# The last batch's q loaded by two transfers of eight outer parts, in a kernel of sliding-window attention and a spectral mix

## The chip, the cores and the metric

The kernel runs on one core of a Trainium2 chip. The metric is the time of one execution on the device in microseconds (us). The core has engines that work side by side: TensorE (PE; its weight loads are listed as PEld), VectorE (DVE), ScalarE (ACT), GpSimd (POOL) and SyncE (SP), and sixteen DMA engines that move data between HBM and the core's memories.

## What is computed

The first part is causal attention in a window of 64 positions, for 8 batches, 8 heads, 576 positions and a head dimension of 64:

```python
scores = (1 / sqrt(D)) * q @ k.transpose(0, 1, 3, 2)
mask = (rel >= 0) & (rel < 64)                 # rel = query position - key position
attn = softmax(where(mask, scores, -1e9))
x = (attn @ v).transpose(0, 2, 1, 3).reshape(B, S, H * D)
```

The second part mixes x in the spectrum of its 64 lowest modes, with one complex 512x512 matrix for each mode:

```python
X = rfft(x, axis=1)[:, :64]
Yr = einsum("bmd,mde->bme", Xr, w_r) - einsum("bmd,mde->bme", Xi, w_i)
Yi = einsum("bmd,mde->bme", Xr, w_i) + einsum("bmd,mde->bme", Xi, w_r)
u = x + irfft(Y, n=576, axis=1)
out = u + maximum(u @ w_ch, 0)
```

The matrices of the modes are 127 matrices of 512x512 in fp32 (the imaginary one of mode 0 isn't needed), by far most of what is read.

## The kernel before

**Stages.** Attention is worked in 36 windows of 512 columns and ends at about 140 us. Between the windows each batch's k, v and q are transposed on TensorE into the layout that the scores need. From 141 us on the 127 matrices are multiplied in, one "half" (16 matmuls, L618) after the other, and between them TensorE does the channel product of x, later the first modes' part of the inverse transform and its product. After the last half the late modes' part is added, rectified and stored (from 390 us).

**The loads.** All loads but one (k of batch 0, on SP) are issued from POOL, which converts them from fp32 to bf16 on the way: `load` (L109) for q, k and v, `load_w` and `load_two` (L136, L141) for one or two matrices. The order is fixed: `refill` (L402) issues, when a batch's k, v or q has been transposed, the load of the same tensor two batches on, and a matrix into each place that is free. Once attention is over, `issue` (L567) loads matrices into a ring of places as they come free. Eight transfers of POOL can be on their way at once: an issue waits until the one eight before it has landed.

**The layout of q, k and v.** Of a batch, [8 heads, 576, 64], each head's 576 positions are cut into 32 runs of RUN = 18 positions. `runs` (L106) gives 128 partitions of two pieces: partition 32*g + p holds run p of head g and of head g + 4. A piece is 18 x 64 = 1,152 elements, 4,608 bytes read, 2,304 written. So a load is one transfer of 256 rows with an outer dimension of 128. The tile `rq` has two buffers; the last batch's q is issued after the q of batch 5 has been transposed.

**The transposes.** `part` (L242) transposes six of the 18 positions of all runs, for both pieces, into a PSUM tile of [128, 6, 128], and a copy (`evac`, L55, on ACT or DVE) puts the columns where they belong: column 32*g + p of position c goes to place g*576 + 18*p + c. `transpose_units` (L234) lists a batch's twelve units of work; those of q are the seventh to ninth, and they run after those of k and v.

Of the kernel before, what the change touches and what calls it, by code (L numbers as in the profile page):

```python
# [11 lines left out]
BF16 = mybir.dt.bfloat16  # L12
# [8 lines left out]
def view(ap, off, dims):  # L21

    return bass.AP(ap.tensor, ap.offset + off, [list(ap.ap[0])] + [list(d) for d in dims])
# [3 lines left out]
def kernel(  # L27
# [10 lines left out]
    nc = tc.nc  # L38
    B, H, S, D = q.shape
# [8 lines left out]
    RUN = S // 32  # L48
# [6 lines left out]
    def evac(o, i, on_act):  # L55

        if on_act:
            return nc.scalar.copy(out=o, in_=i)  # L58
        return nc.vector.tensor_copy(out=o, in_=i)  # L59
# [30 lines left out]
    acons = p1.enter_context(tc.tile_pool(name="acons", bufs=1, side="right"))  # L90
# [10 lines left out]
    RAW = {"k": k, "q": q, "v": v}  # L101

    def raw_tile(which):
        return rawp.tile([128, 2, RUN * D], BF16, name="r" + which)

    def runs(b, which):  # L106
        return RAW[which][b].rearrange("(x g) (p c) d -> (g p) x (c d)", g=4, c=RUN)

    def load(b, which):  # L109
        r = raw_tile(which)  # L110
        nc.gpsimd.dma_start(out=r, in_=runs(b, which))
        raws[b, which] = r


# [63 lines left out]
    with tc.manual_schedule(engines=ALL_FOUR):  # L178
# [3 lines left out]
        with tc.tile_pool(name="tmpf", bufs=1, side="right") as tmp:  # L182
            mo = tmp.tile([128, NM], FP32, name="mo")
            to = tmp.tile([128, NT], FP32, name="to")
            nc.gpsimd.iota(mo, pattern=[[1, NM]], base=0, channel_multiplier=0,
                           allow_small_or_imprecise_dtypes=True)
            nc.gpsimd.iota(to, pattern=[[128, NT]], base=0, channel_multiplier=1,
                           allow_small_or_imprecise_dtypes=True)
            nc.gpsimd.memset(ident, 0.0)
            nc.gpsimd.affine_select(out=ident, in_=ident, compare_op=ALU.not_equal, fill=1.0,  # L190
                                    base=0, pattern=[[-1, 128]], channel_multiplier=1)
            load(0, "q")
            load(0, "v")
            for t0, t1 in ((0, 3), (3, NT)):
                n = t1 - t0
                mt = tmp.tile([128, 2, n * NM], FP32, name="mtf")
                nc.vector.tensor_tensor(out=view(mt, 0, [[NM, n], [1, NM]]), in0=view(mo, 0, [[0, n], [1, NM]]),
                                        in1=view(to, t0, [[1, n], [0, NM]]), op=ALU.mult)
                gen_trig(tmp, mt, n * NM, trigF[:, t0:t1, 0:NM], trigF[:, t0:t1, NM:2 * NM], "f")
                if t0 == 0:  # L200
                    nc.vector.tensor_copy(out=ident_bf, in_=ident)
        nc.scalar.activation(out=spark, in_=ident[:, 0:1], func=ACT_F.Exp)
        raws[0, "k"] = raw_tile("k")
        for c, engine in enumerate((nc.vector, nc.gpsimd, nc.vector)):
            cc = slice(6 * D * c, 6 * D * (c + 1))
            engine.tensor_copy(out=raws[0, "k"][:, :, cc], in_=k_first[:, :, cc])
        load(1, "k")
        for i in range(4):
            half = i % 2
# [24 lines left out]
    def transpose_units(b):  # L234

        rk, rq, rv = (raws.pop((b, which)) for which in "kqv")
        qT = qtp.tile([128, 4, S], BF16, name="qT")
        vT = vtp.tile([128, 4, S], BF16, name="vT")
        kT, vt = kTs[b % 2], vts[b % 2]
        qTs[b] = qT  # L240

        def part(src, dst, c0, on_act):  # L242
            def f():
                ps = ps_misc.tile([128, 6, 128], BF16, name="pst", tag="misc")
                for c in range(6):
                    for hh in range(2):
                        nc.tensor.transpose(out=ps[64 * hh:64 * hh + 64, c, :],  # L247
                                            in_=src[:, hh, (c0 + c) * D:(c0 + c + 1) * D],
                                            identity=ident_bf)
                evac(view(dst, c0, [[S, 4], [RUN, 32], [1, 6]]),  # L250
                     view(ps, 0, [[32, 4], [1, 32], [128, 6]]), on_act)
            return f

        def vback(u):
            def f():
                ps = ps_misc.tile([128, 6, 128], BF16, name="psv", tag="misc")
                for i in range(6):
                    a, j = divmod(6 * u + i, 9)
                    if j == 4:
                        parts = [(0, 64, 2 * a, 512), (64, 64, 2 * a + 1, 0)]  # L260
                    else:
                        parts = [(0, 128, 2 * a + (j > 4), 128 * j - (j > 4) * S)]
                    for r0, n, g, t0 in parts:
                        nc.tensor.transpose(out=ps[r0:r0 + n, i, :],  # L264
                                            in_=vT[:, g, t0:t0 + n], identity=ident_bf)
                evac(view(vt, 6 * u * VW, [[18 * VW, 2], [VW, 6], [1, D]]),
                     view(ps, 0, [[D, 2], [128, 6], [1, D]]), u != 1)
                if u:
                    hs = slice(u - 1, u + 2, 2)
                    nc.vector.tensor_copy(out=vt[64:128, 1, hs, 1:9], in_=vt[64:128, 0, hs, 0:8])  # L270
                    nc.vector.tensor_copy(out=vt[0:64, 1, hs], in_=vt[0:64, 0, hs])
            return f

        return [part(rk, kT, 0, True), part(rk, kT, 6, False), part(rk, kT, 12, True),
                part(rv, vT, 0, False), part(rv, vT, 6, True), part(rv, vT, 12, False),
                part(rq, qT, 0, True), part(rq, qT, 6, False), part(rq, qT, 12, True),
                vback(0), vback(1), vback(2)]

    def head_of(n):
# [143 lines left out]
    with tc.manual_schedule(engines=ALL_FOUR):  # L423
        first = transpose_units(0)
        for j in (0, 1, 2, 6, 7, 8):
            first[j]()
            refill(0, j)
            if j in (2, 8):
                warm_up(3)
        for half in range(2):  # L430
            pp = slice(64 * half, 64 * half + 64)
            nc.vector.tensor_copy(out=band2[pp], in_=band[pp, half, :])
        mask(0, 1)
        scores(0)
        for j in (3, 4, 5):
            first[j]()
            refill(0, j)
            warm_up(2)
        for vt in vts:
            nc.vector.memset(vt[:, 0, :, :, 64:66], 1.0)  # L440
        for j in (9, 10, 11):
            first[j]()
            refill(0, j)
        nc.vector.memset(pso, 1.0)
        nc.vector.tensor_copy(out=ident_r, in_=ident)
    with tc.manual_schedule(engines={E.PE, E.Pool}):
# [9 lines left out]
        def unit(b, j):  # L456
            if b not in units:
                units[b] = transpose_units(b)
            units[b][j]()
            refill(b, j)  # L460
            turned(b, j)

        for w in range(NWIN + 1):
# [5 lines left out]
            n = len(todo)  # L469
# [16 lines left out]
            if w in (NWIN - 4, NWIN - 1):  # L486
                i = (B - 2) % 2 if w == NWIN - 4 else (B - 1) % 2
                spare(kTs[i])
                spare(qtp.tile([128, 4, S], BF16, name="qT"))
            if w in (NWIN - 4, NWIN):  # L490
                i = (B - 2) % 2 if w == NWIN - 4 else (B - 1) % 2
# [363 lines left out]
    def step(f, *a, delta=0):  # L855
        n = {add_z: 2, make_u: 4, last_tile: 2 + (a[-1] is True)}.get(f, 0)
        items.append((lambda: f(*a), delta, n, f is last_tile))
# [20 lines left out]
    for k, (f, delta, n, few) in enumerate(items):  # L878
        i = S_I + k * (T_I - 2 - S_I) // len(items)
# [25 lines left out]
    with tc.manual_schedule(engines=ALL_FOUR):  # L905
# [92 lines left out]
        for k in range(6):  # L998
# [10 lines left out]
                              in_=view(psys[0], 0, [[2 * B, NC], [2, B], [1, 2]]))  # L1009
# [78 lines left out]
```

## Time and profile before

| | us |
|---|---|
| median of 3 runs | 425.43 |
| the runs | 425.22, 425.43, 598.11 |
| profiled execution | 425.65 |
| its span | 423.8 |
| PE busy | 352.3 (83%) |
| DVE busy | 189.2 (45%) |
| ACT busy | 159.8 (38%) |
| POOL busy | 81.6 (19%) |

The span goes from the first instruction to the last; the profiled execution's own time is 1.85 us more. A busy share is an average over stages with different limits. A view names an instruction by its engine, the line of the code and the tiles that it writes and reads (`wms<-in_moe_w_r_dram` is a load of matrices into the tile wms). Queue q0 holds the transfers issued from POOL, q1 those from SP, q8 the fetches of instructions. The 16 DMA engines' busy time is given as a share; packets of one engine overlap a little, so a full stretch shows slightly over 1.

The trace also holds, for each transfer, sixteen reports of landing, one from each DMA engine, in the order of time; they don't tell which engine sent them. Four transfers, first report and the others from it (us):

| transfer, issued at | first report | eighth | ninth | last |
|---|---|---|---|---|
| rq, batch 0, 1.60 | 8.46 | +0.2 | +0.2 | +0.7 |
| rq, batch 7, 87.78 | 104.44 | +0.5 | +1.4 | +2.4 |
| wls, 190.59 | 207.56 | +0.9 | +3.1 | +4.5 |
| wms, the last, 375.98 | 384.51 | +1.0 | +4.6 | +5.9 |

### The profile page before, as it was taken

How to read it: one execution, taken by the hardware profiler on the slowest of the kernel's cores; microseconds unless marked ns; L12 is line 12 of the kernel's file. 1: busy time of each engine (PE TensorE's matmuls, PEld its weight loads, DVE VectorE, ACT ScalarE, POOL GpSimd, SP SyncE). 2: the span in 40 equal slices, each digit the busy share in tenths (PEclk: the TensorE clock that was granted, in tenths of full speed). 3: DMA queues.
4: the chain of work that ended last, by engine and by line, in shares of the span. 5: the costliest groups of instructions: out<-in, count | busy, mean ns of one | idle time of the engine just before them, and what ended most of it. 6: DMA issues, size and time to landing. Idle time of an engine off the chain costs nothing.

```text
span 423.8 us, 11438 instructions
## 1 busy us (share of the span) xinstructions
PE 352.3 (83%) x5156; PEld 233.6 (55%) x5185; DVE 189.2 (45%) x359; ACT 159.8 (38%) x267; POOL 81.6 (19%) x146
## 2 busy tenths in 40 slices
PE   7799999999997779866669587767789899998994
PEld 3466656656654567644446455545556565554451
DVE  6676775766764001634332351121104345340895
ACT  5565766767754100122102110110023343330863
POOL 6322222221031130411112012120121112200000
PEclk9999999999999555966756656666579999999997
DMA  8999999999999999999999999999999999995598
GB/s 212 211 214 212 214 212 212 213 213 213 214 214 214 213 215 261 215 214 214 215 214 213 215 213 215 215 213 215 213 215 214 214 213 211 214 214 106 203 370 320
DMA packets 29920, 92.55 MB, mean 218 GB/s; under 512 B 2352, under 2 KB 2352, under 8 KB 29872
## 3 DMA queue, kind: packets, MB, share of 16 engines
q0 software_dynamic: 24624, 81.21, 95.9%
q1 hardware_dynamic: 5248, 10.62, 6.8%
q8 instruction: 40, 0.66, 0.6%
q14 instruction: 8, 0.07, 0.0%
HBM read 162.53 MB, written 9.44 MB: 406 GB/s over the span
## 4 chain that ended last, share of the span: by engine, by line
PE 42%; DMA 39%; DVE 7%; issue 5%; ACT 3%; POOL 0%; DVEq 0%; POOLq 0%; ACTq 0%
DMA wms<-in_moe_w_r_dram 20%; DMA wms<-in_moe_w_i_dram 19%; PE psy L618 7%; PE pso L343 6%; PE pst L247 5%; PE psv L264 3%; PE psx L365 3%; PE pss L963 3%; DVE x_sb L351 2%; PE pss L956 2%; PE pss L300 2%; PE pss L319 2%; PE psy L903 2%; DVE vT L59 2%; PE psf L800 1%
## 5 line engine op out<-in xcount | busy, mean ns | idle before, releaser
L759 PE MATMUL psz<-wch,xT 128*128 128x512 f32 x144 | 65.0, 594 | 0.0
L753 DVE CAST xT<-pxt 128x1024 fp32r<-128x1024 bf16 x18 | 22.0, 1224 | 78.0 <-PE pxt L748 78.0
L762 ACT CAST Z<-psz 128x1024 fp32r<-128x1024 f32 x18 | 18.2, 1012 | 102.2 <-PE psz L759 94.5
L325 ACT ACTIVATE et<-pss 128x512 bf16<-128x512 f32 x72 | 39.2, 599 | 13.7 <-PE pss L319 13.7
L618 PE MATMUL psy<-XQ,wls 128*128 128x16 bf16 x560 | 22.0, 192 | 23.7 <-DMA wls<-in_moe_w_r_dram 14.2
L759 PEld LDWEIGHTS psz<-wch,xT 128*128 128x128 f32 x144 | 37.4, 287 | 5.9
L618 PE MATMUL psy<-XQ,wms 128*128 128x16 bf16 x624 | 25.1, 192 | 17.9 <-DMA wms<-in_moe_w_i_dram 12.7
L618 PEld LDWEIGHTS <-wls 128*128 128x128 bf16 x560 | 19.5, 106 | 33.8 <-DMA wls<-in_moe_w_r_dram 17.4
L618 PEld LDWEIGHTS <-wms 128*128 128x128 bf16 x624 | 21.4, 103 | 30.2 <-DMA wms<-in_moe_w_i_dram 15.3
L343 PE MATMUL pso<-vt,et 128*64 128x65 bf16 (+1 forms) x576 | 32.3, 203 | 3.5 <-DVE x_sb L351 1.6
L811 DVE TENSOR_TENSOR Z<-pse,Z 128x1024 fp32r<-128x1024 f32 x16 | 19.6, 1225 | 29.3 <-PE pse L800 29.3
L343 PEld LDWEIGHTS <-et 128*64 128x64 bf16 (+1 forms) x576 | 22.2, 109 | 14.2 <-issue 6.7
L351 DVE TENSOR_TENSOR x_sb<-pso,rcp 128x640 bf16<-128x640 f32 x32 | 26.3, 822 | 0.9
L618 PE MATMUL psy<-XQ,wt 128*128 128x16 bf16 x560 | 20.5, 192 | 4.8 <-DMA wt<-in_moe_w_i_dram 2.3
L618 PEld LDWEIGHTS <-wt 128*128 128x128 bf16 x560 | 18.3, 104 | 11.2 <-DMA wt<-in_moe_w_i_dram 4.3
L59 DVE CAST YT<-psy 128x256 fp32r<-128x256 f32 x6 | 2.5, 424 | 42.0 <-PE psy L618 32.7
L59 DVE COPY vT<-pst 128x768 bf16<-128x768 bf16 x16 | 15.3, 958 | 12.9 <-PE pst L247 11.3
L981 ACT ACTIVATE pss<-pss 128x512 f32<-128x512 f32 x35 | 18.5, 581 | 4.7 <-PE pss L963 4.1
L300 PE MATMUL pss<-band,ident_bf 64*64 64x512 bf16 x120 | 16.5, 396 | 0.0
L264 PE MATMUL psv<-ident_bf,vT 128*128 128x128 bf16 (+1 forms) x160 | 15.6, 226 | 0.6 <-DVE vT L59 0.6
L58 ACT COPY vt<-psv 128x768 bf16<-128x768 bf16 x16 | 12.9, 807 | 8.3 <-PE psv L264 8.2
L58 ACT COPY qT<-pst 128x768 bf16<-128x768 bf16 x16 | 12.9, 813 | 6.4 <-PE pst L247 6.4
(191 smaller groups left out, 605.7 us busy)
## 6 DMA issues: line engine op xcount, KB each, us to landing
wt<-in_moe_w_i_dram POOLq DMA_DIRECT2D x19, 512.0 KB, 20.4
wt<-in_moe_w_r_dram POOLq DMA_DIRECT2D x16, 512.0 KB, 19.4
wls<-in_moe_w_r_dram POOLq DMA_DIRECT2D x8, 1024.0 KB, 21.8
wms<-in_moe_w_i_dram POOLq DMA_DIRECT2D x7, 1024.0 KB, 22.2
wms<-in_moe_w_r_dram POOLq DMA_DIRECT2D x7, 1024.0 KB, 21.6
wls<-in_moe_w_i_dram POOLq DMA_DIRECT2D x6, 1024.0 KB, 21.3
rq<-in_q_dram POOLq DMA_DIRECT2D x8, 576.0 KB, 15.3
rv<-in_v_dram POOLq DMA_DIRECT2D x8, 576.0 KB, 13.8
```

What stands on the lines that cost most here:

```text
L58: return nc.scalar.copy(out=o, in_=i)
L59: return nc.vector.tensor_copy(out=o, in_=i)
L247: nc.tensor.transpose(out=ps[64 * hh:64 * hh + 64, c, :], in_=src[:, hh, (c0 + c) * D:(c0 + c + 1) * D], identity=ident_bf)
L264: nc.tensor.transpose(out=ps[r0:r0 + n, i, :], in_=vT[:, g, t0:t0 + n], identity=ident_bf)
L300: nc.tensor.matmul(out=pss[(2 * w + hh) % 3][64 * half:64 * half + 64, :], lhsT=ident_bf[pp, pp], rhs=view(band[pp], 128 * half, [[0, WIN ...
L325: nc.scalar.activation(out=et[:, hh, :], in_=pss[(2 * w + hh) % 3], func=ACT_F.Exp, scale=EX_SCALE)
L343: nc.tensor.matmul(out=pso[po, hh, block(b, i // 2) * VW:block(b, i // 2) * VW + D + 1], lhsT=et[pk, hh, col:col + 64], rhs=vt[pk, 1 - f % ...
L351: nc.vector.tensor_tensor(out=view(x_sb, b * NT * DM + g * D, [[4 * D, 2], [DM, NT], [1, D]]), in0=view(pso, 0, [[512, 2], [VW, NT], [1, D]]),
L618: nc.tensor.matmul(out=view(psy, off + 2 * B * e, [[1, 2 * B]]), lhsT=w[:, c, 128 * e:128 * e + 128], rhs=XQ[:, m // HM, c, :, 1 - im:3 - ...
L753: nc.vector.tensor_copy(out=o, in_=i)
L759: nc.tensor.matmul(out=psz[s][:, j, :], lhsT=xts[s % 2][0][:, j, 128 * c:128 * c + 128], rhs=wch[:, c, :], start=(c == 0), stop=(c == NC - 1))
L811: nc.vector.tensor_tensor(out=z, in0=ps, in1=z, op=ALU.add)
```

## The change

Only the last batch's q is touched (B - 1, "q"). Its one transfer becomes two, one for each piece x (heads 0 to 3, heads 4 to 7). The source of a half is given as 8 outer parts of 16 rows, the rows of a part eight runs apart: partition 16*i + j now holds run i + 8*j of the four heads, counted through, where it held run 32*g + p in that order. The copies after the transposes undo that (`halved`): column 16*i + j goes to place (i + 8*j)*18 + c, by a write of the same 768 elements in another order.

Before the first half, between the two and after the second, a small transfer copies two rows of 16 elements for each of 2, 8 and 6 outer parts from k of batch 0 into a new tile `aside` that nothing reads.

```diff
+    BY_HALF = (B - 1, "q")
+    aside = acons.tile([16, 3, 16], BF16, name="aside")
+
+    def spread(ap, off, parts, n, m):
+
+        return bass.AP(ap.tensor, ap.offset + off, [[RUN * D, parts], [parts * RUN * D, n], [1, m]])
+
+    def step(x, n):
+
+        nc.gpsimd.dma_start(out=aside[:2 * n, x, :], in_=spread(k[0], 0, n, 2, 16))
+
     def load(b, which):
         r = raw_tile(which)
-        nc.gpsimd.dma_start(out=r, in_=runs(b, which))
+        if (b, which) == BY_HALF:
+            for x in range(2):
+                step(x, (2, 8)[x])
+                nc.gpsimd.dma_start(out=r[:, x, :], in_=spread(RAW[which][b], x * H // 2 * S * D, 8, 16, RUN * D))
+            step(2, 6)
+        else:
+            nc.gpsimd.dma_start(out=r, in_=runs(b, which))
         raws[b, which] = r
...
-        def part(src, dst, c0, on_act):
+        def part(src, dst, c0, on_act, halved=False):
...
-                evac(view(dst, c0, [[S, 4], [RUN, 32], [1, 6]]),
-                     view(ps, 0, [[32, 4], [1, 32], [128, 6]]), on_act)
+                to, at = ([S, 4], [RUN, 32]), ([32, 4], [1, 32])
+                if halved:
+                    to, at = ([8 * RUN, 16], [RUN, 8]), ([1, 16], [16, 8])
+                evac(view(dst, c0, [*to, [1, 6]]), view(ps, 0, [*at, [128, 6]]), on_act)
...
-                part(rq, qT, 0, True), part(rq, qT, 6, False), part(rq, qT, 12, True),
+                *(part(rq, qT, 6 * i, i != 1, (b, "q") == BY_HALF) for i in range(3)),
```

## The prediction

> **What bounds the kernel.** I read the page first, then the chain in its last stage, then stretches around the end of the weight stream, then the transfers one by one. From the page (DMA share and GB/s are in 40 slices of 10.6 us):
>
> ```profile
> DMA  8999999999999999999999999999999999995598
> GB/s 212 211 214 212 214 212 212 213 213 213 214 214 214 213 215 261 215 214 214 215 214 213 215 213 215 215 213 215 213 215 214 214 213 211 214 214 106 203 370 320
> ...
> q0 software_dynamic: 24624, 81.21, 95.9%
> ...
> q8 instruction: 40, 0.66, 0.6%
> ...
> PE 42%; DMA 39%; DVE 7%; issue 5%; ACT 3%; POOL 0%; DVEq 0%; POOLq 0%; ACTq 0%
> ```
>
> The transfers run at one rate, 211 to 215 GB/s, from the start to slice 36; in slice 37 the rate halves to 106. That slice holds the end of the weight stream. The chain there (start, us, what):
>
> ```profile
> 361.37 13.62 DMA wms<-in_moe_w_r_dram
> 375.06 0.90 issue
> 375.98 14.40 DMA wms<-in_moe_w_i_dram
> ```
>
> The last weight lands at 390.39, TensorE takes it up at 390.43, and 33.4 us of arithmetic and stores follow to 423.8. So the stream's end sets the span. Cutting the stretch before it (us, busy time of PE, PEld, DVE, ACT, POOL, clock, DMA share, GB/s):
>
> ```profile
> 370.00:380.00 10.00, 9.28 (x89) 5.36 (x92) 4.65 (x4) 3.95 (x4) 0.53 (x1) 1.00 1.06 213
> 380.00:384.50 4.50, 4.10 (x46) 2.27 (x46) 0.84 (x2) 0.58 (x1) 0.00 (x0) 1.00 1.02 206
> 384.50:390.40 5.90, 4.68 (x47) 2.50 (x45) 0.39 (x1) 0.35 (x1) 0.00 (x0) 1.00 0.43 86
> ```
>
> In the last 5.9 us the 16 DMA engines are busy to 0.43, against 1.06 before (packets overlap, so full is a little over 1). The trace keeps for each transfer sixteen landing reports, one per engine. For the last weight, counted from the first report at 384.51, they come at 0, 0.1, 0.1, 0.2, 0.2, 0.2, 0.6, 1.0 and then at 4.6, 4.9, 5.0, 5.0, 5.1, 5.2, 5.3, 5.9. **Eight engines are about 5 us ahead of the other eight.** In the first load (rq, issued at 1.60) all sixteen report within 0.7 us. The eight late ones don't speed up when the others are done: their last two transfers report last at 387.98 and 390.39, 2.41 us apart, against 2.45 in the full stream. So each engine has its own rate and its own queue, and the stream ends with the most loaded engine.
>
> The cause is in q8: 40 fetches of instructions of 16 KB, at 15.4 us to 392.8 us, each 0.89 to 1.07 us. Their durations repeat with a period of eight (893, 892, 949, 945, 935, 974, 974, 1072 ns, then 893 again), as if eight engines took turns: 39 before 390 us, five for most of the eight, 5 x 0.94 = 4.7 us, which is the lag seen. I call these eight heavy, the others light.
>
> **The change, part by part.** *Removed:* one transfer of 576 KB (256 rows of 2,304 bytes, 16 an engine). Successive loads of that kind in the first 31 us report first at 14.06, 16.88, 19.64, 22.41, 25.21, 28.03, 30.80: 2.79 us of each engine. *Added:* two halves of 128 rows each. The trace of before has no transfer whose outer dimension is under 16, so how many engines take a half is bounded by sixteen (nothing moves) and fewer. I take eight, one outer part per engine: every transfer before has an outer dimension of 128, and sixteen reports spread evenly. Then a half is 16 rows on each of eight engines, 2.79 us again; two halves on the same eight are 5.58 there and 0 on the others. If parts are dealt to engines by turns, the second half begins 8 (first half) + 8 (small one) = 16 parts after the first, so both fall on the same eight, and the small ones on the rest; 2 + 8 + 8 + 8 + 6 = 32 parts in all leave the turn where it was.
>
> The Trainium skill, "DMA: Bandwidth & Descriptors", section "Why a DMA increments its semaphore by 16 and not by 1", says that a transfer uses the largest number up to 16 that divides the slowest dimensions of both sides, and that one with fewer than 16 is put on consecutive engines from a cursor that goes round. By it the halves take eight engines; no run here shows it yet. The same section tells of copies that got all 16 anyway; by that the halves would change nothing, which is a rival below.
>
> *If the eight are the light ones:* these end 2.79 later, the heavy ones 2.79 earlier. The latest light one ends at 385.51 + 2.79 = 388.3, the latest heavy one at 390.39 - 2.79 = 387.6, plus 0.2 at most for four tiny rows and four more reports (the 4-byte reports take some 0.02 us). The end of the stream moves from 390.4 to 388.35: **-2.0 us**. That is not all that balance could give: 0.43 x 5.90 = 2.5 us of sixteen engines' work is left at 384.5, so even levelling would end at 384.5 + 2.5 / 1.06 = 386.9, -3.5 us.
>
> *Can TensorE follow?* From 333 to 363 us it starts on a weight up to 2.6 us after its landing, so there it is itself the limit. It stands still for landings for 0.94 us at 331.43 and 2.4 us in all from 365 to 390.43. So 2.0 us earlier landings can be taken up, but hardly more than 3.
>
> *Where the halves sit in the queue:*
>
> ```profile
> 84.29 0.70 POOL L111 DMA_DIRECT2D rv<-in_v_dram  x1 [2.62 <-PE pst L247]
> 84.99 0.57 POOL L138 DMA_DIRECT2D wt<-in_moe_w_i_dram  x1
> 87.78 0.70 POOL L111 DMA_DIRECT2D rq<-in_q_dram  x1 [2.23 <-PE pst L247]
> 88.84 0.56 POOL L138 DMA_DIRECT2D wt<-in_moe_w_i_dram  x1 [0.36 <-DMA wt<-in_moe_w_i_dram]
> 91.28 0.54 POOL L138 DMA_DIRECT2D wt<-in_moe_w_r_dram  x1 [1.88 <-DMA rq<-in_q_dram]
> ```
>
> Five issues stand for one of 0.70: four more of 0 to 0.7 us on POOL, which is idle for some 2 us between issues here. Behind them are the weight loads from 88.84 on, which wait for the landing of the load eight before them. The five take five of these eight places, so the loads behind come up to some 10 us later: the first at 99 instead of 88.8, the second at 102.3, the third at 104.2. The heavy engines finish what they have at 103 to 103.9, the light ones the second half at 107.2 to 107.7. A starved engine begins about 2.5 us after the issue (issue at 355.00, first report at 359.94, less 2.45), so the three loads are at hand and no engine runs dry: 0 us. If the cover failed, each microsecond that a light engine is empty would be one at the end. TensorE first needs the weight of 88.84 at 149.8, 40 us after its landing.
>
> *The q itself* lands at 106.8; half by half it is there by 107.7. Its transposes begin at 115.94: 8 us to spare, 0 us. *The copies out of PSUM* (three, ACT 0.81 us, DVE 0.96 us) have the same 768 elements and the same innermost six; a strided read could cost or save a few tenths, and they lie 270 us before the end: 0 us.
>
> **Sum.** Span 423.8 - 2.0 = 421.8. The profiled execution took 425.65, 1.85 more than its span, the median of the runs is 425.43: 425.43 - 2.0 = **423.4**.
>
> **Rivals.** *Wrong eight (slower).* The reports carry no engine's name, so nothing in the trace says which eight are light, or where the turn stands at the start. One heavy engine among the eight decides: it ends 2.79 later with nothing taken off. The least late heavy one would end at 384.5 + 4.6 + 2.79 = 391.9 (+1.5 us), the latest at 393.2 (+2.8 us): 426.9 to 428.2. For it speaks that of sixteen places where a run of eight may begin only one fits; against it, that light and heavy are exactly eight each, which is what two halves on eight can level, so a run that fits exists if the heavy ones stand side by side, as their fixed order suggests. *All sixteen take part.* Then the halves are the old load in another order of rows, with three tiny transfers: 0 to +0.3 us, 425.4 to 425.7. For it: every transfer in the trace reports from sixteen. *Starved queue:* the places run out where I found them just enough; 1 to 3 us back, 424.5 to 427.
>
> The skill's same page, section "Latency and other measured facts", says that engines 7 and 15 are usually slower than the others. By it two engines would be late and a half on engine 7 would give the wrong-eight case. The trace shows eight late within 1.3 us of each other, not two.
>
> **Chances.** Light eight 0.53; wrong eight 0.32; all sixteen 0.10; starved or other 0.05. The light case alone spans 422.5 (TensorE takes up all of the 3 us that it can) to 424.4 (the light engines lag 1 us more); with the wrong eight's upper end, the range is 422.6 to 428.3. Two per cent is 8.5 us, about what a measurement of this kernel can tell from no change; no case above reaches it. I leave 0.01 beyond it on the fast side and 0.03 on the slow side, for a form of transfer that this trace doesn't show.
>
> **What would show it.** Right: the last weight's sixteen reports within some 2.6 us instead of 5.9, the last of them at about 388.4; the DMA share of the stream's last 6 us well over 0.43; right after the halves, at 107 to 110 us, the light eight the late ones, by up to 4.7 us, and the two groups drawing together from there to the end. Wrong: a spread of 8 us or more at the end (a heavy engine got a half), or a spread of 5.9 as before (all sixteen took part). An empty stretch of DMA at 100 to 112 us would show the starved queue. What would make the number wrong with the mechanism right: halves on eight engines that take other than 2.79 us each.

## The result, and the profile after

The changed kernel takes 428.09 us (median), 2.5 us more than the kernel before in the same comparison (425.62): ratio 1.0063, 95% interval 1.0047 to 1.0079. The forecast was 423.4. One execution of the kernel before took 598.11 us, far from all others, and is not part of the ratio. The time is that of the "wrong eight" rival, 426.9 to 428.2.

The page of the changed kernel, in the lines that were read before (share and GB/s in 40 slices, now of 10.66 us):

```profile
DMA  8999999999999999999999999999999999993598
GB/s 209 212 213 212 213 214 211 214 213 207 211 213 214 214 215 259 215 214 213 215 213 215 214 214 214 213 216 214 213 215 214 214 209 209 213 213 80 197 371 320
...
q0 software_dynamic: 25040, 81.21, 95.6%
...
q8 instruction: 40, 0.66, 0.6%
```

The same megabytes go through the queue, but the slow slice 36 (counting from 0) has fallen from 106 to 80 GB/s: the tail in which some engines work alone is longer. The stretches show it (us, busy time of PE, PEld, DVE, ACT, POOL, clock, DMA share, GB/s):

```profile
380.00:384.50 4.50, 4.19 (x45) 2.47 (x45) 1.82 (x2) 1.90 (x3) 0.00 (x0) 1.00 1.08 218
384.50:390.40 5.90, 5.02 (x50) 2.65 (x49) 0.39 (x1) 0.90 (x2) 0.00 (x0) 1.00 0.50 100
390.40:393.00 2.60, 2.25 (x27) 1.17 (x28) 0.00 (x0) 0.00 (x0) 0.00 (x0) 1.00 0.13 25
```

Where the stream was over at 390.4 before, a share of 0.13 of the engines goes on here. The last weight's reports, from the first at 385.58, come at 0, 0, 0.2, 0.6, 1.4, 1.5, 1.5, 1.9, 2.2, 2.2, 2.2, 2.3, 2.9 and then 6.8, 6.9, 7.3. **Three engines** end it, at 392.84 instead of 390.39. The other heavy engines have indeed moved forward, into the middle group; it didn't help, as the last one decides. The chain's last piece of the stream (start, us, what):

```profile
378.72 14.12 DMA wms<-in_moe_w_i_dram
```

378.72 + 14.12 = 392.84. From there to the end of the span, 426.3, are 33.5 us, as before (33.4).

How many engines took a half can be read around 102 us. The queue on POOL there (start, us, engine, line, what; in brackets the idle time before it):

```profile
86.64 0.58 POOL L119 DMA_DIRECT2D aside<-in_k_dram  x1
89.36 0.61 POOL L126 DMA_DIRECT2D rq<-in_q_dram  x1 [2.14 <-PE pso L363]
91.83 0.62 POOL L119 DMA_DIRECT2D aside<-in_k_dram  x1 [1.86 <-DMA rq<-in_q_dram]
94.36 0.60 POOL L126 DMA_DIRECT2D rq<-in_q_dram  x1 [1.90 <-DMA wt<-in_moe_w_r_dram]
97.13 0.56 POOL L119 DMA_DIRECT2D aside<-in_k_dram  x1 [2.17 <-DMA rk<-in_k_dram]
99.58 0.57 POOL L156 DMA_DIRECT2D wt<-in_moe_w_i_dram  x1 [1.90 <-DMA wt<-in_moe_w_r_dram]
```

The second half, issued at 94.36, was reported first at 102.29 by engines that carried nothing; eight reports lie within 3.0 us of that and eight at +5.0, 5.1, 5.2, 5.4, 5.5, 7.1, 7.3 and 7.4. So eight engines carried it. The matrix load ahead of these transfers had been reported by light engines from 101.57 to 102.2 and by heavy ones up to 104.56: among the eight carriers, five ended at 107.3 to 107.8 and three at 109.4 to 109.7. The five stand 5.6 us behind five of the light reports of that load, so they are light, and the three behind them are heavy; which heavy report belongs to which of the three can't be told.

### The profile page after: what moved, and what is told of

It reads as the page before. It is cut to its first block, busy times and chain, and to the rows that moved or that the text cites. A ratio compares the mean times of both kernels' runs of the same rounds, so it can differ in the third digit from the quotient of the medians.

```text
span 426.3 us, 11473 instructions
## 1 busy us (share of the span) xinstructions
PE 356.7 (84%) x5185; PEld 234.2 (55%) x5185; DVE 188.7 (44%) x359; ACT 159.9 (38%) x267; POOL 84.1 (20%) x150
## 4 chain that ended last, share of the span: by engine, by line
DMA 48%; PE 35%; DVE 7%; issue 4%; ACT 2%; POOL 1%; DVEq 0%; POOLq 0%; ACTq 0%
DMA wms<-in_moe_w_i_dram 22%; DMA wms<-in_moe_w_r_dram 20%; DMA wt<-in_moe_w_i_dram 6%; PE pso L363 6%; PE pst L265 5%; PE psy L638 4%; PE psv L284 3%; PE psx L385 3%; PE pss L983 2%; DVE x_sb L371 2%; PE pss L976 2%; PE pss L320 2%; PE pss L339 2%; DVE vT L59 2%; ACT vt L58 1%
## 5 line engine op out<-in xcount | busy, mean ns | idle before, releaser
L923 PE MATMUL psy<-trigF,ident_bf 128*128 128x512 bf16 x46 | 17.8, 450 | 0.0
```

## The experiments

**Theory A:** the parts of a transfer are dealt by turns to consecutive engines, and the loss is that three heavy engines got a half. **Theory B:** a transfer of eight parts always takes the same engines, wherever the turn stands. **Theory C:** the loss is the price of the added transfers, not of their place. Theory D (the round begins elsewhere in each execution) came with the marks.

### Other places in the turn

The first experiment moves the halves by three places one way (`off5`), the second by three the other way (`off15`):

```diff
-                step(x, (2, 8)[x])
+                step(x, (5, 8)[x])        # off5; off15: (15, 8)[x]
...
-            step(2, 6)
+            step(2, 3)                    # off5; off15: step(2, 9), aside 30 rows
```

> The small transfers have 5, 8 and 3 parts in place of 2, 8 and 6: both halves begin three places later in the turn. Theory A (in the changed kernel the halves fell on five light and three heavy engines, and parts are dealt by turns): if the eight heavy engines stand side by side, a shift by three places goes either to all light or to two light and six heavy. All light: the last weight lands at about 389.0 (light 385.5 + 2.79 + 0.7 for four more landing reports of 0.18 us), 1.4 us before 390.4, time 424.2. Six heavy: last landing as in the changed kernel, 392.8, but six reports of the last weight late instead of three, time 428.1. Theory B (the place of the halves doesn't depend on the small transfers, a transfer of eight parts always takes the same engines): 428.1, three reports late. Theory C (the loss is the price of the added transfers, not of the place): 428.1, three reports late.

> The small transfers have 15, 8 and 9 parts: both halves begin three places earlier in the turn than in the changed kernel (15 = 2 - 3 + 16). Theory A: the mirror of the run with 5, 8 and 3 parts. Whichever of the two isn't all light has six heavy engines: 428.1 with six late reports; the other 424.2 with a spread of the last weight's reports of 3 us or less. Theories B and C: 428.1, three late reports.

`off5` took 428.28 us (before, in the same comparison: 425.74; ratio 1.0064, 1.0052 to 1.0076), `off15` 427.75 (1.0049, 1.0036 to 1.0062). Neither was all light. Right after the second half, `off5` has two early and six late among its eight carriers (4.8 and 4.8 us behind the first report of that half, then 6.0 to 7.5): two light, six heavy, as theory A had for one of the two. `off15` has six and two (5.1 to 5.7; then 7.4, 7.4), and at the end of the stream exactly two late reports, at 7.0 behind the first, where the changed kernel has three. So the place follows the small transfers, which leaves B out. But a step of three from five light led to six, not eight: **the eight heavy engines don't stand side by side**, and that part of the expectation fell. (In `off5` seven reports of the last weight stand 2.0 us or more behind the first, not six, and the first itself comes only at 389.75. The reports name no engine, so I can't say which the seventh is.) Its last weight lands at 380.01 + 13.54 = 393.55 (the chain's last piece of the stream). Some of that may be another loss: from 345 to 350 us `off5` moves 152 GB/s where the changed kernel moves 206, so that some of its engines stood empty there. In this execution, which is the slowest of the five (428.85), TensorE's granted clock was 0.50 from 335 to 340 us and 0.83 from 340 to 345, where the profiled execution of the changed kernel has 1.00 in both, and the load that had to wait for TensorE was issued at 348.63 instead of 344.88. How much of the 2.5 us of `off5` belongs to this was not told apart.

The times tell why a count of three, six or two heavy engines hardly matters: one is enough, and the price is that of one.

### The added transfers without the move

`all16` gives the halves sixteen outer parts and keeps the small transfers; `smalls` keeps the old load of q and puts the three small ones ahead of it:

```diff
 # all16
-... spread(RAW[which][b], x * H // 2 * S * D, 8, 16, RUN * D))
+... spread(RAW[which][b], x * H // 2 * S * D, 16, 8, RUN * D))
...
-                    to, at = ([8 * RUN, 16], [RUN, 8]), ([1, 16], [16, 8])
+                    to, at = ([16 * RUN, 8], [RUN, 16]), ([1, 8], [8, 16])
 # smalls
             for x in range(2):
                 step(x, (2, 8)[x])
-                nc.gpsimd.dma_start(out=r[:, x, :], in_=spread(...))
             step(2, 6)
+            nc.gpsimd.dma_start(out=r, in_=runs(b, which))
...
-                *(part(rq, qT, 6 * i, i != 1, (b, "q") == BY_HALF) for i in range(3)),
+                *(part(rq, qT, 6 * i, i != 1, False) for i in range(3)),
```

> The halves have an outer source dimension of sixteen in place of eight, with the copies adapted; the small transfers stay. Theory A: each half takes all sixteen engines, so nothing is moved between them; what is left is the cost of the added transfers, four more landing reports of 0.18 us on each engine, read from the changed kernel at 102 us: last landing 390.4 + 0.7 = 391.1, time 426.1 to 426.3, spread of the last weight's reports 5.9 as before. Theory C: 428.1 here too.

> The three small transfers alone, ahead of the old single load of q. Theory A: three more reports of 0.18 us on each engine, +0.5 us, 425.9 to 426.1. Theory C: near 428.

`all16` took 425.95 us, ratio 1.0012 (0.9997 to 1.0027); its last weight landed at 390.66 with a spread of 5.33. `smalls` took 425.78, ratio 1.0003 (0.9994 to 1.0011). Neither differs from before beyond its interval, and both cost less than I expected. (The profiled execution of `smalls` is the slowest of its eleven, 426.33; in it the last weight landed at 390.99, 0.6 us later than before, which is the size expected.) Theory C is out: with the same number of transfers the loss is gone as soon as all sixteen engines carry the halves.

### Marks: which places are light

`label` is the kernel before with eighteen small transfers among the late matrix loads, into a tile that is dead by then:

```diff
+    marks = list(enumerate([2] * 8 + [3] + [2] * 8 + [13]))
...
+                if nw >= UP and marks:
+                    x, n = marks.pop(0)
+                    nc.gpsimd.dma_start(out=ident[:2 * n, 7 * x:7 * x + 7], in_=bass.AP(
+                        q.tensor, q[0].offset, [[RUN * D, n], [n * RUN * D, 2], [1, 7]]))
```

> The kernel before, with one small transfer of two rows a part ahead of each of eighteen late matrix loads: eight of 2 parts, one of 3, eight of 2, one of 13 (48 parts). It marks the engines: each small transfer's data packets show at what lag the engines stand that it was dealt to, two by two, and by the odd shift of 3 the pairs of the second pass overlap those of the first. It also tells the theories apart. Theory A (parts go round by turns, and the eight heavy engines have fixed places in the round): each pass shows every engine once; counted from where the turn stands, places 0 to 4 are light and 10 to 12 heavy, two of 5 to 9 and one of 13 to 15 are light. That follows from the light engines among the eight of a half, five (2, 8, 6), two (5, 8, 3) and six (15, 8, 9), and from the two engines marked first in the changed kernel, both light. Theory B (no turn; a transfer of two parts always takes the same engines): all sixteen pairs show the same two lags. Theory D (the round is there but begins elsewhere in each execution): the pairs show a mix that doesn't fit those counts. Time within 1 us of before.

It took 425.63 us (one run; before 425.68). In the trace's packets an engine that has a part of a mark writes one packet of 56 bytes, the others one of 8 bytes. So the packet's time gives the lag of the two engines that a mark was dealt to, behind the first report of that mark:

```
places    lag, us           places    lag, us
 0,  1    0.12  0.48         3,  4    0.32  0.40
 2,  3    0.69  1.55         5,  6    1.34  2.43
 4,  5    0.02  4.39         7,  8    0.00  0.81
 6,  7    4.39  0.00         9, 10    1.50  1.95
 8,  9    0.55  3.92        11, 12    2.66  2.90
10, 11    2.65  4.04        13, 14    2.78  2.90
12, 13    3.59  3.77        15,  0    0.40  0.56
14, 15    0.73  3.10
first pass                  second pass, after a mark of three parts
```

The mark of three parts (places 0 to 2) and the one on places 1 and 2 that ends the second pass lie at 0.3 to 1.0. From the first to the second pass the lags shrink: the marks take places from the eight transfers that may be on their way, and the light engines wait for issues (around 340 us the first reports of two matrices stand up to 3.6 us apart, where 2.45 is the full rate). The order stays: in the second pass the eight light ones are within 1.0, the heavy ones at 1.3 and more. A few packets of neighbouring marks lie within some tens of nanoseconds of each other and were told apart by the count of two for each mark and by the other pass. **Light are places 15, 0, 1, 2, 3, 4, 7 and 8; heavy are 5, 6 and 9 to 14.** That gives five light in places 2 to 9, two in 5 to 12, six in 15 to 6, which are the counts of the three kernels above; it leaves out B and D. And no eight places in a row hold more than six light ones: the change's form, two transfers of eight parts, can't have only light engines anywhere in the turn.

### The same idea on the light places, and its mirror

With six parts for 96 partitions and two parts for the other 32, the layout of the change stays and all q can go to light places (`lit62`); other sizes of the small transfers put the same transfers on heavy places (`hvy62`). `early(1)` draws one matrix load ahead, so that the heavy engines have work meanwhile; `aside` grows to [30, 5, 16]:

```diff
             for x in range(2):
-                step(x, (2, 8)[x])
-                nc.gpsimd.dma_start(out=r[:, x, :], in_=spread(...))
-            step(2, 6)
+                for p0, parts in ((0, 6), (6, 2)):
+                    nc.gpsimd.dma_start(out=r[16 * p0:16 * (p0 + parts), x, :], in_=bass.AP(
+                        RAW[which].tensor, RAW[which][b].offset + (x * H // 2 * S + p0 * RUN) * D,
+                        [[RUN * D, parts], [8 * RUN * D, 16], [1, RUN * D]]))
+                    if p0 == 0:
+                        step(1 + 2 * x, 2)          # hvy62: 6
+                if x == 0:
+                    early(1)
+                    step(2, 6)                      # hvy62: 2
+                else:
+                    step(4, 7)                      # hvy62: 9
...
+            if (b, which) == (B - 1, "k"):
+                step(0, 15)                         # hvy62: 9
```

> By the marks, counted from where the turn stands, places 15, 0, 1, 2, 3, 4, 7 and 8 are light and 5, 6 and 9 to 14 heavy, so no eight places in a row are all light. Here each half goes in two transfers, 96 partitions by six parts to places 15 to 4 and 32 partitions by two parts to places 7 and 8; small transfers of 15, 2, 6, 2 and 7 parts move the turn between them, and one matrix load is drawn ahead of the second half so that the heavy engines have work. Each light engine takes 32 rows, no heavy one any. Theory A: light ones +2.79 us, heavy ones -2.79 us, last weight at about 388.3 in place of 390.4, span 421.8, time 423.7 beside 425.7 of before, ratio 0.995; last weight's reports within 3 us. Theory C (added transfers cost, place is nothing): 428 or more, since there are nine transfers in place of five. If the heavy engines starve for want of issued loads, up to 2 us of the gain goes.

> The mirror: the same transfers of q in the same order, but the small ones have 9, 6, 2, 6 and 9 parts, so that the six parts fall on places 9 to 14 and the two on 5 and 6, all heavy. Theory A: the heavy ones end 2.79 us later, the light ones 2.79 earlier; last weight at 393.2, all eight heavy reports late (in the changed kernel three were), time 428.3 to 428.8. Theory C: the same time as the run with the light places.

`lit62` took 424.97 us (before 425.67; ratio 0.9980, 0.9965 to 0.9996), `hvy62` 428.76 (1.0065, 1.0041 to 1.0088). Only the sizes of the small transfers differ between the two, and they stand 3.8 us apart, on both sides of the kernel before. In `hvy62` the last weight lands at 393.60 with eight late reports, 4.1 to 5.7 behind the first. Its last stretches, in the columns used above:

```profile
384.50:390.40 5.90, 5.64 (x60) 3.31 (x55) 0.66 (x2) 0.94 (x2) 0.00 (x0) 1.00 0.83 166
390.40:393.00 2.60, 2.09 (x25) 1.07 (x23) 0.00 (x0) 0.00 (x0) 0.00 (x0) 1.00 0.43 87
```

So the direction is as theory A has it; but `lit62` got 0.7 of the 2.0 us. The GB/s row of `lit62` tells where the rest went:

```profile
GB/s 213 211 212 214 213 214 213 212 211 209 189 215 213 213 214 262 214 213 215 213 216 213 215 214 214 216 213 214 213 216 213 215 212 215 213 215 144 206 370 318
```

In slice 10 (105.8 to 116.4 us) the rate falls to 189, where before has 214: engines stood empty. Nine small and large transfers take nine of the places of the queue; the matrix for the heavy engines was issued only here:

```profile
105.08 0.61 POOL L126 DMA_DIRECT2D rq<-in_q_dram  x1 [2.30 <-DMA wt<-in_moe_w_i_dram]
105.68 0.56 POOL L119 DMA_DIRECT2D aside<-in_k_dram  x1
106.21 1.17 POOL L166 DMA_DIRECT2D wt<-in_moe_w_r_dram  x2
```

The heavy engines had landed the matrix ahead of it at 107.4 at the latest, and reported this one from 111.06: 3.7 us for 2.45 us of work, 1.2 us lost. `lit62b` draws one more matrix load ahead of the last two-part transfer. `lit6` makes the same move with fewer transfers: the six-part transfers go to places 15 to 4, the other 32 partitions to all sixteen engines.

```diff
 # lit62b, from lit62
                     if p0 == 0:
+                        if x == 1:
+                            early(1)
                         step(1 + 2 * x, 2)
 # lit6, from the changed kernel
             for x in range(2):
-                step(x, (2, 8)[x])
-                nc.gpsimd.dma_start(out=r[:, x, :], in_=spread(..., 8, 16, RUN * D))
-            step(2, 6)
+                nc.gpsimd.dma_start(out=r[0:96, x, :], in_=spread(..., 6, 16, RUN * D))
+                if x == 1:
+                    early(1)
+                step(1 + x, 10 + x)
+            nc.gpsimd.dma_start(out=r[96:128], in_=runs(b, which)[96:128])
```

(and, as in `lit62`, a small transfer of 15 parts ahead of the last batch's k; `lit6` copies q out of PSUM in two pieces for each part).

> As the run on light places with six and two parts, with one more matrix load drawn ahead of the last two-part transfer. There the heavy engines landed the drawn matrix at 107.4 at the latest and the next one, issued only at 106.2, from 111.1 on: about 1.2 us and more of empty heavy engines. Theory A with this cause of the missing gain: the heavy engines stay busy, the last weight lands 0.5 to 1.2 us before 389.7, time 424.0 to 424.5. If the missing gain was lost elsewhere (reports of nine transfers on the light engines): 425.0 again.

> Fewer transfers: each half's first 96 partitions by six parts to the light places 15 to 4, the other 32 partitions of both halves in one transfer of all sixteen engines, small transfers of 15, 10 and 11 parts; the copies of q out of PSUM in two pieces each. Six light engines take 36 rows (+20, 3.5 us), the two other light ones and the heavy ones 4 (-12, -2.1 us). Theory A: latest light 385.5 + 3.5 = 389.0, latest heavy 390.4 - 2.1 = 388.3; time 424.3 beside 425.7 of before. Theory C: above 426.

`lit62b` took **424.01 us** beside 425.91 before: ratio **0.9959** (0.9945 to 0.9973). `lit6` took 424.52, ratio 0.9969 (0.9958 to 0.9981). Both beat the kernel before and the changed one. The row of `lit62b`, and its last stretches:

```profile
GB/s 207 212 212 214 213 213 212 213 213 208 209 216 213 213 215 261 216 212 216 213 215 213 214 214 213 215 214 213 215 213 215 213 213 213 213 214 147 208 370 318
```

```profile
380.00:384.50 4.50, 4.34 (x48) 2.38 (x47) 0.02 (x1) 0.59 (x1) 0.00 (x0) 1.00 1.06 214
384.50:390.40 5.90, 4.92 (x48) 2.77 (x48) 0.64 (x2) 0.35 (x1) 0.00 (x0) 1.00 0.50 101
390.40:393.00 2.60, 2.52 (x15) 1.34 (x14) 1.30 (x2) 1.30 (x3) 0.00 (x0) 1.00 0.02 6
```

Slice 10 is back at 209, and the slow slice 36 at 147 GB/s, from 106 before and 80 after the change. The chain's last piece of the stream:

```profile
374.91 13.78 DMA wms<-in_moe_w_i_dram
```

The middle stretch has the same share, 0.50, as in the changed kernel, and means something else: here the engines end nearly together, the last weight lands at 388.69 with its sixteen reports within 1.36 us, and the next stretch is down to 0.02. A share over a stretch doesn't tell half the engines all the time from all the engines half the time; the reports and the stretch behind it do. In `lit6` the last weight lands at 389.22 (389.0 expected).

## Why the prediction was wrong

- **What bounds the kernel: right.** Every landing of the last weight measured here moved the span by the same amount: 392.84 for 390.39 (+2.45) made +2.5 us of span, 388.69 (-1.7) made -1.6 (422.2 for 423.8).
- **Eight light and eight heavy engines: right,** and shown by the marks. That the fetches of instructions make them heavy was argued in the prediction from count and length; the trace of the kernel before bears it out in time. The lags of a matrix's eight late reports, each taken from the mean of the eight early ones, add up to 25.4 us for the load issued at 172.89 and to 31.9 for the one issued at 257.12. Between them lie six fetches (at 191.4, 207.9, 225.4, 235.6, 255.0 and 270.1). The sum grows by 0.9 to 1.2 us across each, about the length of a fetch (at the last with an overshoot of 0.7 at one load), and else moves by no more than 0.3 from load to load; the spread of the early eight stays at 0.84 to 0.88. So the fetches delay the late group alone. No kernel here changed their number.
- **A half takes eight engines, both halves the same eight: right.** The rule of the Trainium skill on the number of engines and on the cursor that goes round ("DMA: Bandwidth & Descriptors", "Why a DMA increments its semaphore by 16 and not by 1") agrees with the traces: eight carriers, and places that shift with the sizes of the small transfers. The case in which all sixteen take part did not come up.
- **2.79 us a half on an engine: right.** Five carriers ended 5.6 us after the load ahead of them for 5.58 predicted.
- **The eight are the light ones: the step that failed.** It was put at 0.53 with no line of the trace behind it; the changed kernel has three heavy ones among its eight. The rival had the price right: 393.2 for the latest heavy one, 392.84 measured, and 428.2 for 428.09. I had argued against this rival that a run of eight that fits exists if the heavy engines stand side by side "as their fixed order suggests". The fetches' fixed order in time doesn't say where the engines stand in the turn, and they don't stand side by side. An even count of light and heavy was no reason to put the light case above one half: in all sixteen positions of the turn there is none in which it holds.
- **The sign given for this case, a spread of 8 us or more at the end: not met, though the case was this one.** The spread was 7.3. It was 8.0 for the matrix issued at 351.29; the next was issued only at 356.30, the first reports of the two stand 3.6 us apart instead of 2.45, and the spread fell to 6.9. The light engines without a half had run so far ahead that they waited for an issue, which the sign didn't reckon with.
- **The queue: "no engine runs dry" was not quite so, and it cost nothing here.** Behind the halves the first reports of three matrices come at 104.82, 107.44 and 110.44, 2.62 and 3.00 us apart instead of 2.45: the light engines without a half stood empty for some 0.7 us in all. They had 5 us and more to spare to the heavy ones, so the end didn't feel it. With the nine transfers of `lit62` the heavy engines stood empty for 1.2 us, and one matrix load more made good most of the gain that was missing (0.70 us under the kernel before in `lit62`, 1.90 in `lit62b`).
- **The added transfers, 0.2 us at most: the times show no more, the reason was thin.** `all16`, with four transfers more than before, took 425.95 us beside 425.74, and `smalls`, with three, 425.78. But the trace of the changed kernel shows 0.18 us of an idle engine's time for each small transfer, where the prediction had 0.02 for a report.
- **What balance is worth: right in size.** The -2.0 us forecast for the light eight is -1.9 in `lit62b`, which needs other transfers than the change has.

## What to carry to other kernels

Where one stream sets the end and its transfers are spread over all DMA engines, look at the spread of the sixteen landing reports of one transfer: if it grows along the kernel, the stream runs at the pace of the most loaded engines, and the spare time of the others can be used. To move work between engines one has to know which they are; small transfers that mark the engines cost nothing here (425.63 beside 425.68, one execution of each) and tell it in one run, where shifting by guess gave three losses. And a transfer that carries nothing still takes a place in the queue: draw real loads in between.

## What the runs showed of the hardware

- An engine that has no part in a transfer still gets packets and still reports. The page counts small packets:

```profile
DMA packets 29920, 92.55 MB, mean 218 GB/s; under 512 B 2352, under 2 KB 2352, under 8 KB 29872
```

  In the changed kernel:

```profile
DMA packets 30336, 92.55 MB, mean 217 GB/s; under 512 B 2768, under 2 KB 2768, under 8 KB 30288
```

  The 416 more are 32 rows of the small transfers (32 bytes each), 64 reports (four more transfers, sixteen each), and 320 packets of 4 bytes, some 9 ns each: 16 for each of eight engines in each half, and 64 for the small ones. So each engine gets as many packets as the carriers have rows.
- The light and heavy engines are not two blocks in the turn: heavy are places 5, 6 and 9 to 14, counted from where the turn stood at the start, the same in the eight kernels here that show it.
- Three added transfers cost nothing that can be measured (ratio 1.0003, 0.9994 to 1.0011), although each holds the reports of an idle engine apart by 0.18 us.
